# Queries of four token chunks in one layout, loaded in two transfers by heads

## The chip, the cores and the metric

The kernel runs on one core of a Trainium2 chip. The metric is the device time of one execution in microseconds; the time before is the median of 11 runs.

## The reference

A recurrent attention with decay (retention) is followed by a feed-forward layer with a product of two branches, and all of it is computed in float32 by the reference:

```python
for t in range(S):
    state = gamma * state + einsum('bhd,bhe->bhde', k[:, :, t], v[:, :, t])
    y[:, :, t] = scale * einsum('bhd,bhde->bhe', q[:, :, t], state)
x = y.transpose(0, 2, 1, 3).reshape(B * S, H * D)
out = ((x @ w1) * (x @ w2) @ w3) @ w_out
```

There are 4 batches, 8 heads, 768 tokens per batch and a head size of 64, so x is 3072 by 512; w1 and w2 are 512 by 1024, w3 is 1024 by 1024, w_out 1024 by 512. `gamma` is one constant per head.

## The kernel before

The tokens are cut into 24 chunks of 128. Within a chunk the recurrence becomes matmuls: scores (keys against queries, L437), a mask product on DVE (`am`, L442), outputs (values and the running state, L477 to L480), and an update of the state (`kv`, L460 to L469). Heads are taken in four pairs (`NP`), so that two heads of 64 fill the 128 partitions. The decays are put into exponentials: `VS` scales the values as they are cast to float16 into `VP`, `YS` scales the outputs as they are written to `XT` (L485), which is x transposed, ready for the feed-forward matmuls.

The two last weights are multiplied beforehand: `W3O` = w3 @ w_out (`w3_mm_columns`, `w3_mm`), from transposes of w3. Then each block of 256 tokens takes `x @ w1` and `x @ w2` (L508), their product `HT`, and `HT @ W3O` (L534).

The order on every engine is the order in which the program is written; nothing is rearranged later. All loads are issued by SP on one queue, in program order, and most are 512 KB. The order of the loads is: four w3 column blocks and four w_out blocks in turn, four w3 row blocks, then q, k and v of the first pair of chunks (`load_pair(0)`), the four row blocks of w1, q and k of the second pair, a row block of w2, v of the second pair, the rest of w2, and then the chunks from 4 on. `load_pair` puts two neighbouring tokens into one partition, so a contiguous run is 2 x 64 floats, 512 B. With this layout token 2i + t of a pair of chunks lies in partition i; in the first four chunks the order of keys and values within the chunk follows from it (`pair_casts`), and so do the mask `keep2` and the position table `if_i`.

The stretch around the change is written by hand, from L674 to L779. It runs in this order:

- `q_cast(0)` on POOL (L327), then the casts of k (L313) and v (L318), for the first pair, shared by POOL and DVE.
- On PE the rest of `w3_mm` (L293), the query transposes of chunks 0 and 1 (`q_transposes(0)`, L366) with two copies back on DVE (`qT`, L228), the key transposes of chunks 0 and 1 (L421) with copies back into `KP` (L426 and L230, ACT), scores, outputs and state of these chunks.
- On POOL the casts of W1 row blocks 0 and 1 (L687); on ACT the casts of blocks 2 and 3.
- `by_rows` (L724) multiplies the first 256 tokens of `XT` with w1 one row block at a time, first for chunk 0's columns, then for chunk 1's, then for whole blocks. Between blocks 2 and 3 stand the query transposes of chunks 2 and 3 (`q_transposes(1)`), their copies on DVE, and chunk 2's key transposes (`transposes(2)`), the last in the midst of block 3.
- Then scores and outputs of chunks 2 and 3 between the row blocks of w2, the first products `HT`, and a loop over chunks 4 to 23 (`step`), in which a queue of feed-forward units is drawn down by fixed costs.

Tiles are kept in named PSUM banks (`psA0`, `psA1`, `psY`, `psK`, `psT`, three of `psF`), and a new tile under a name waits until the last one is read.

Of the kernel before, what the change touches and what calls it, by code (L numbers as in the profile page):

```python
# [9 lines left out]
FP = mybir.dt.float32  # L10
HP = mybir.dt.float16
AF = mybir.ActivationFunctionType
MULT = mybir.AluOpType.mult
# [5 lines left out]
def kernel(  # L19
# [11 lines left out]
    nc = tc.nc  # L31
    B, H, S, D = q.shape
    C = 128
# [5 lines left out]
    NP = H // 2  # L39
# [21 lines left out]
    def dma_in(dst, src):  # L61
        nc.sync.dma_start(dst, src)  # L62

    chunk_in = {}
    q_in = {}
    pair_in = {}

    def load_pair(m, names="qkv"):

        b, c = divmod(2 * m, NCH)  # L70
        for nm, src in (("q", q), ("k", k), ("v", v)):
            if nm not in names:
                continue
            if nm == "q":
                t = ld.tile([128, 2 * 512], FP, tag="q64", name="q64", bufs=3)
                q_in[m] = t
            else:
                t = new_stage()
                pair_in[nm, m] = t
            dma_in(  # L80
                t[:, :].rearrange("p (h x) -> p h x", x=2 * D),
                src[b, :, c * C : (c + 2) * C, :].rearrange("h (p t) d -> p h (t d)", t=2),
            )

    def load_chunk(n):
        if n >= NSTEP:
            return
        b, c = divmod(n, NCH)
        tiles = []
        if c % 2 == 0:  # L90

            t = ld.tile([128, 2 * 512], FP, tag="q64", name="q64", bufs=3)
            dma_in(
                t[:, :].rearrange("p (h x) -> p h x", x=2 * D),
                q[b, :, c * C : (c + 2) * C, :].rearrange("h (p t) d -> p h (t d)", t=2),
            )
            q_in[n // 2] = t
        for nm, src in (("k", k), ("v", v)):
            t = ld.tile([128, 512], FP, tag=nm + "32", name=nm + "32")
            dma_in(  # L100
                t[:, :].rearrange("p (h d) -> p h d", d=D),
                src[b, :, c * C : (c + 1) * C, :].rearrange("h i d -> i h d"),
            )
            tiles.append(t)
        chunk_in[n] = tiles
# [29 lines left out]
        w3c_st.append(load_w3_columns(i))  # L135
        wo_st.append(load_wo(i))
    w3_st = {f: load_rows(moe_w3, f) for f in range(4, 8)}
    load_pair(0)
    w1_st = [load_rows(moe_w1, d) for d in range(4)]
    load_pair(1, "qk")  # L140
    w2_st = [load_rows(moe_w2, 0)]
    load_pair(1, "v")
    w2_st += [load_rows(moe_w2, d) for d in range(1, 4)]
# [43 lines left out]
    for p in range(NP):  # L187
        nc.scalar.activation(YS[:, p, :], if_f[:, :], AF.Exp, scale=LGP[:, p : p + 1])

    keep2 = const.tile([128, 128], FP, name="keep2")  # L190
    nc.gpsimd.memset(keep2[:, :], 1.0)
    for t in range(2):
        r = slice(t * 64, t * 64 + 64)
        nc.gpsimd.affine_select(
            out=keep2[r, :], in_=keep2[r, :], compare_op=mybir.AluOpType.is_ge, fill=0.0,
            base=-t, pattern=[[1, 2], [2, 64]], channel_multiplier=-2,
        )

    ip2_i = const.tile([128, 2, H], mybir.dt.int32, name="ip2_i")
# [5 lines left out]
    zero(KP[0])  # L205
    zero(KP[1])

    for i in (1, 2):
        nc.gpsimd.memset(VP[i][:, :, :, :].rearrange("p a b c -> p (a b c)").bitcast(FP), 0.0)
    nc.gpsimd.memset(GS[:, :, :], 0.0)  # L210
# [4 lines left out]
    XT = {}  # L215
# [10 lines left out]
    def cast_to(dst, src, on_dve):  # L226
        if on_dve:
            nc.vector.tensor_copy(dst, src)  # L228
        else:
            nc.scalar.copy(dst, src)  # L230
# [11 lines left out]
    def bank(tag, shape, dtype, name):  # L242
        return (ps_t if tag == "psT" else ps_at).tile(shape, dtype, tag=tag, name=name)
# [43 lines left out]
    def w3_mm(f, between=None, at=4):  # L287
        t = w3t.pop(f)
        ps = ps_f.tile([128, DM], FP, tag="psF", name="psW")
        for g in range(8):  # L290
            if g == at and between:
                between()
            nc.tensor.matmul(  # L293
                ps[:, :], lhsT=t[:, g * 128 : (g + 1) * 128], rhs=WO[g // 2][:, g % 2, :],
                start=(g == 0), stop=(g == 7),
            )
        cast_to(W3O[f][:, :], ps[:, :], False)
# [27 lines left out]
    def q_cast(m):  # L325
        q16 = att.tile([128, 1024], HP, tag="q16", name="q16")
        nc.gpsimd.tensor_copy(  # L327
            q16[:, :].rearrange("i (t h d) -> i h t d", t=2, d=D),
            q_in.pop(m)[:, :].rearrange("i (h t d) -> i h t d", t=2, d=D),
        )  # L330
        q16s[m] = q16

    def casts(n):
        if n >= NSTEP:
            return
        k32, v32 = chunk_in.pop(n)
        if n % 2 == 0:
            q_cast(n // 2)
        k16 = att.tile([128, 512], HP, tag="k16", name="k16", bufs=3)
        nc.gpsimd.tensor_copy(k16[:, :], k32[:, :])  # L340
        vp = VP[n % 3]

        for r in range(2):
            nc.gpsimd.tensor_tensor(  # L344
                vp[:, :, r, r * 64 : r * 64 + 64],
                v32[:, :].rearrange("j (p s e) -> j p s e", s=2, e=64)[:, :, r, :],
                VS[:, :].rearrange("j (p s) -> j p s", s=2)[:, :, r].unsqueeze(2).broadcast_to((128, NP, 64)),
                MULT,
            )
        k16s[n] = k16  # L350

    def q_transposes(m, later=False):

        if m >= DT0 // 2:
            return
        q16 = q16s.pop(m)
        if m == 0:
            ps = ps_at.tile([128, NP, 2, 128], HP, tag="psA0", name="psTq")
        elif m == 1:
            ps = ps_at.tile([128, NP, 2, 128], HP, tag="psA1", name="psTq")  # L360
        else:
            ps = ps_f.tile([128, NP, 2, 128], HP, tag="psF", name="psTq")
        for p in range(NP):
            for t in range(2):
                c0 = t * 512 + p * 128
                nc.tensor.transpose(ps[:, p, t, :], q16[:, c0 : c0 + 128], ident16[:, :])  # L366

        def back(c, on_dve=True):
            qT = att.tile([128, NP, 128], HP, tag="qT", name="qT", bufs=4)
            cast_to(  # L370
                qT[:, :, :].rearrange("p a (t i) -> p (a t) i", t=2),
                ps[:, :, :, c * 64 : (c + 1) * 64].rearrange("p a t i -> p (a t) i"), on_dve,
            )
            qTs[2 * m + c] = qT

        if later:
            return back
        back(0)
        back(1)

    def by_dma(n):

# [23 lines left out]
    def transposes(n, tag="psT"):  # L406
        if n >= NSTEP:
            return
        if by_dma(n):
            kT, kp = kTs.pop(n), KP[n % 2]  # L410
            nc.scalar.copy(kp[0:64, :, 0, :], kT[0:64, :, :])  # L411
            nc.scalar.copy(kp[64:128, :, 1, :], kT[64:128, :, :])  # L412
            return
        transposes_front(n, tag)
        transposes_back(n)
# [56 lines left out]
    def outputs(n, tag="psY"):  # L472
        am, vp = ATs.pop(n), VP[n % 3]
        c = n % NCH
        ps = bank(tag, [128, NP, 128], FP, "psY")
        for p in range(NP):
            nc.tensor.matmul(ps[:, p, :], lhsT=vp[:, p, 0, :], rhs=am[:, p, 0, :], start=True, stop=False)  # L477
            nc.tensor.matmul(ps[:, p, :], lhsT=vp[:, p, 1, :], rhs=am[:, p, 1, :], start=False, stop=(c == 0))  # L478
            if c > 0:
                nc.tensor.matmul(ps[:, p, :], lhsT=Tst[0][:, p, :], rhs=queries(n, p), start=False, stop=True)  # L480
        if n % 2 == 0:
            XT[n // 2] = xpool.tile([128, NP, 256], HP, tag="xt", name="xt")

        order = "p a (t i) -> p a t i"
        nc.vector.tensor_tensor(  # L485
            XT[n // 2][:, :, n % 2 * C : (n % 2 + 1) * C].rearrange("p a (i t) -> p a t i", t=2),
            ps[:, :, :].rearrange(order, t=2), YS[:, :, :].rearrange(order, t=2), MULT,
        )


# [138 lines left out]
    def cast_w(W, st, d, on_dve):  # L629
        cast_to(W[d][:, :], st[d][:, :], on_dve)  # L630
# [40 lines left out]
    w3_transpose(5)  # L671
    cast_w3(6, w3_st[6])
    cast_w3(7, w3_st[7])
    q_cast(0)  # L674
    pair_casts(0, False, "k")
    pair_casts(1, False, "k")
    pair_casts(0, False, "v")
# [3 lines left out]
    w3_mm(5, lambda: w3_transpose(7))  # L681
    pair_casts(0, True, "k")
    pair_casts(1, True, "k")
    q_transposes(0)
    pair_casts(0, True, "v")
    for r in (0, 1):
        nc.gpsimd.tensor_copy(W1[r][:, :], w1_st[r][:, :])  # L687
    w3_mm(6, lambda: transposes(0), 3)
    transposes(1, "psK")
    scores(0)  # L690
    cast_w(W1, w1_st, 2, False)

    def chunk1_scores():
        first.append(kv(0, "psT"))
# [2 lines left out]

    first = []
    w3_mm(7, chunk1_scores)
    Tst[0] = first[0]  # L700
    outputs(1, "psT")
    Tst[0] = kv(1, "psK", nc.vector)
    cast_w(W1, w1_st, 3, False)
    q_cast(1)

    ffn = [Ffn(a, b - a) for a, b in zip(bounds, bounds[1:])]
    NT = len(ffn)
# [27 lines left out]
        pair_casts(n, False, "k")  # L735
        pair_casts(n, True, "k", nc.scalar)
    by_rows(W1, ps, 2)
    q_back = q_transposes(1, True)
    q_back(0)
    q_back(1)  # L740
    by_rows(W1, ps, 3, blocks=(0, 3))
    transposes(2)
    by_rows(W1, ps, 3, blocks=(3, 8))
    transposes_front(3, "psK")
    pa = [hold[i // 2][:, i % 2 * 512 : i % 2 * 512 + 512].rearrange("p (a n) -> p a n", a=2) for i in range(4)]
    nc.gpsimd.tensor_copy(W2[0][:, :], w2_st[0][:, :])
# [85 lines left out]
```

## Time and profile before

| | |
|---|---|
| median of 11 runs | 195.01 us (194.67 to 196.93) |
| the profiled execution | 194.85 us |
| its span in the trace | 193.0 us |
| PE busy | 184.1 us (95%) |
| DVE, ACT, POOL busy | 117.4, 99.9, 85.7 us |
| granted TensorE clock | 0.998 |
| moved by DMA | 40.54 MB |

A span runs from the first to the last instruction of the profiled execution, and the 1.85 us that the time is longer lie around it. Lines such as `23.68 1.56 DVE L313 CAST ... x2` give the start and the length in us, the engine, the line of the kernel, the operation, what is written from what, the shape, and how many instructions were merged. A bracket holds the engine's idle time before it and what ended that. A line number can be a helper's (L228 and L230 are DVE's and ACT's copies, L62 issues a load).

### The profile page before, as it was taken

To read this page: it belongs to the slowest core of one execution; us is meant where nothing else is said; L and a number is where in the kernel's file an instruction comes from. 1 tells how busy PE (TensorE), PEld (TensorE's weight loads), DVE (VectorE), ACT (ScalarE), POOL (GpSimd) and SP (SyncE) were. 2 spreads that over 40 slices of the span, in tenths; PEclk is the share of its full clock that TensorE was granted. 3 is DMA by queue.
4 is the path that set the end of the run, shared out by engine and by line. 5 is a ranking of instruction groups with operands and counts; after the bars stand their busy time and mean duration, and the time that the engine had idled before them with its cause. 6 is when DMAs were issued, how large, how long until landed. Compare 5 with 4: busy or idle time off the path is not lost.

```text
span 193.0 us, 4697 instructions
## 1 busy us (share of the span) xinstructions
PE 184.1 (95%) x1777; PEld 139.6 (72%) x1777; DVE 117.4 (61%) x220; ACT 99.9 (52%) x192; POOL 85.7 (44%) x146
## 2 busy tenths in 40 slices
PE   6689999879999999999999999999999999999993
PEld 2335657677797789777877797788777877887752
DVE  3226598599587758656665676565656665753220
ACT  6578565772454464454635463555355545533322
POOL 7600378638872658457153652862426432200000
PEclk9999999999999999999999999999999999999999
DMA  5999999999899999999999999979979931111104
GB/s 194 369 389 395 296 402 323 357 302 201 182 222 221 240 205 239 115 266 219 221 251 251 184 225 218 204 160 267 199 177 209 198 94 21 58 54 54 38 27 156
DMA packets 85031, 40.54 MB, mean 210 GB/s; under 512 B 61329, under 2 KB 80017, under 8 KB 85009
## 3 DMA queue, kind: packets, MB, share of 16 engines
q1 hardware_dynamic: 85008, 40.25, 87.7%
q8 instruction: 14, 0.23, 0.6%
q14 instruction: 9, 0.07, 0.2%
HBM read 29.36 MB, written 6.29 MB: 185 GB/s over the span
## 4 chain that ended last, share of the span: by engine, by line
PE 81%; DMA 10%; POOL 3%; SPq 1%; DVE 1%; issue 1%; ACT 1%; POOLq 0%; DVEq 0%
PE psF L508 39%; PE psO L534 21%; DMA stg<-in_v_dram 5%; DMA stg<-in_moe_w_dram 5%; PE psA L437 5%; PE psY L477 3%; PE psY L478 3%; PE psF L724 2%; PE psY L480 2%; PE psK L460 2%; POOL vp L318 2%; SPq L62 1%; PE psG L508 1%; PE psO L551 1%; PE psG L724 1%
## 5 line engine op out<-in xcount | busy, mean ns | idle before, releaser
L508 PE MATMUL psF<-xt,w 128*128 128x256 f16 (+1 forms) x736 | 85.0, 266 | 0.0
L508 PEld LDWEIGHTS <-w 128*128 128x128 f16 x768 | 68.2, 98 | 7.2
L524 DVE TENSOR_TENSOR ht<-pa,psF 128x256 f16<-128x256 f32 x88 | 36.6, 417 | 22.7 <-PE psF L508 12.8
L518 ACT COPY pa<-psF 128x256 f32<-128x256 f32 x84 | 31.3, 373 | 33.7 <-PE psF L508 33.3
L442 DVE TENSOR_TENSOR am<-psA,keep 128x512 f16<-128x512 f32 x48 | 31.0, 685 | 20.9 <-PE psA L437 20.8
L534 PE MATMUL psO<-w3o,ht 128*128 128x512 f16 x184 | 43.3, 379 | 0.0
L469 POOL TENSOR_TENSOR t<-s,GS 128x512 f16<-128x512 f32 x15 | 19.3, 1283 | 33.2 <-DVE s L468 33.1
L539 ACT ACTIVATE osb<-psO 128x512 f32<-128x512 f32 x23 | 13.8, 599 | 35.6 <-PE psO L534 35.6
L534 PEld LDWEIGHTS <-ht 128*128 128x128 f16 x184 | 17.9, 98 | 16.9 <-DVE ht L773 0.2
L344 POOL TENSOR_TENSOR vp<-v,VS 128x256 f16<-128x256 f32 x40 | 23.8, 614 | 8.6 <-DMA v<-in_v_dram 5.0
L327 POOL CAST q<-q 128x1024 f16<-128x1024 f32 x12 | 12.7, 1056 | 28.6 <-DMA q<-in_q_dram 28.6
L485 DVE TENSOR_TENSOR xt<-psY,YS 128x512 f16<-128x512 f32 x24 | 17.8, 742 | 4.0 <-PE psY L480 3.6
L477 PE MATMUL psY<-am,vp 128*128 128x128 f16 x96 | 16.8, 219 | 0.6 <-ACT kp L230 0.4
L478 PE MATMUL psY<-am,vp 128*128 128x128 f16 x96 | 16.7, 219 | 0.6 <-DVE vp L318 0.6
L437 PEld LDWEIGHTS <-kp 128*128 128x128 f16 x192 | 12.5, 98 | 4.9 <-DVE kp L228 0.4
L340 POOL CAST k<-k 128x512 f16<-128x512 f32 x20 | 12.2, 611 | 5.9 <-DMA v<-in_v_dram 2.2
L468 DVE TENSOR_TENSOR s<-psK,t 128x512 f32<-128x512 f32 x16 | 11.0, 689 | 3.0 <-PE psK L460 2.7
L251 DVE COPY w3t<-psW 128x1024 f16<-128x1024 f16 x8 | 5.5, 690 | 10.6 <-PE psW L259 8.2
L411 ACT COPY kp<-kT 64x512 f16<-64x512 f16 x17 | 10.5, 620 | 1.9 <-DMA kT<-k 1.5
L437 PE MATMUL psA<-qTd,kp 128*128 128x128 f16 x144 | 11.1, 219 | 0.0
L480 PE MATMUL psY<-qTd,t 128*128 128x128 f16 x60 | 10.8, 219 | 0.0
L412 ACT COPY kp<-kT 64x512 f16<-64x512 f16 x17 | 10.5, 617 | 0.4
(82 smaller groups left out, 190.2 us busy)
## 6 DMA issues: line engine op xcount, KB each, us to landing
stg<-in_moe_w_dram SPq DMA_DIRECT2D x16, 512.0 KB, 7.8
q<-in_q_dram SPq DMA_DIRECT2D x12, 512.0 KB, 5.7
out_dram<-osb SPq DMA_DIRECT2D x23, 256.0 KB, 3.9
k<-in_k_dram SPq DMA_DIRECT2D x20, 256.0 KB, 5.2
v<-in_v_dram SPq DMA_DIRECT2D x20, 256.0 KB, 5.5
stg<-in_moe_w_out_dram SPq DMA_DIRECT2D x4, 512.0 KB, 7.8
stg<-in_k_dram SPq DMA_DIRECT2D x2, 512.0 KB, 10.7
stg<-in_v_dram SPq DMA_DIRECT2D x2, 512.0 KB, 8.2
```

Of the source, the lines that this page charges most:

```text
L344: nc.gpsimd.tensor_tensor(vp[:, :, r, r * 64 : r * 64 + 64], v32[:, :].rearrange("j (p s e) -> j p s e", s=2, e=64)[:, :, r, :], VS[:, :]. ...
L437: nc.tensor.matmul(ps[:, i, r, :], lhsT=kp[:, p, r, :], rhs=queries(n, p), start=True, stop=True)
L442: nc.vector.tensor_tensor(am[:, half * 2 : half * 2 + 2, :, :].rearrange("j p s i -> j (p s) i"), ps[:, :, :, :].rearrange("j p s i -> j ( ...
L469: eng.tensor_tensor(t16[:, :, :], s32[:, :, :], GS[:, :, :], MULT)
L477: nc.tensor.matmul(ps[:, p, :], lhsT=vp[:, p, 0, :], rhs=am[:, p, 0, :], start=True, stop=False)
L478: nc.tensor.matmul(ps[:, p, :], lhsT=vp[:, p, 1, :], rhs=am[:, p, 1, :], start=False, stop=(c == 0))
L480: nc.tensor.matmul(ps[:, p, :], lhsT=Tst[0][:, p, :], rhs=queries(n, p), start=False, stop=True)
L485: nc.vector.tensor_tensor(XT[n // 2][:, :, n % 2 * C : (n % 2 + 1) * C].rearrange("p a (i t) -> p a t i", t=2), ps[:, :, :].rearrange(orde ...
L508: nc.tensor.matmul(ps[:, i * w : (i + 1) * w], lhsT=W[d][:, (f + i) * 128 : (f + i + 1) * 128], rhs=XT[self.tok0 // TB][:, d, c0 : c0 + w] ...
L518: nc.scalar.copy(self.pa[f][:, :], ps[:, :])
L524: nc.vector.tensor_tensor(self.HT[:, f : f + TB // self.width, :].rearrange("p f n -> p (f n)"), self.pa.pop(f)[:, :], ps[:, :], MULT,)
L534: nc.tensor.matmul(psO[:, :], lhsT=self.HT[:, f, tb * 128 : (tb + 1) * 128], rhs=W3O[f][:, :], start=(f == 0), stop=(f == 7),)
```

## The change

The queries of chunks 0 to 3 (512 tokens) are loaded by two transfers, `load_q4(0)` for heads 0 to 3 and `load_q4(1)` for heads 4 to 7, four neighbouring tokens in a partition, so a contiguous run is 1 KB. Both stand ahead of the first k; the second pair's q load goes. The first half is cast on POOL, the second on ACT (`q4_cast`). Eight PE transposes for each half (`q4_transposes`) stand where `q_transposes(0)` stood, with a copy back for each chunk and half: six on DVE, and on ACT those of chunks 2 and 3 for the second half. Query columns within a chunk now come in another order, so the mask `keep2` and the decay table take it (`YS4`, made by two POOL copies), and `outputs` writes `XT` with a stride of 4 instead of 2. `q_transposes(1)` and `q_cast(1)` go; `transposes(2)` now stands ahead of the whole of W1 row block 3; the cast of W1 row block 2 stands behind `w3_mm(7)`; chunk 0's key transposes use bank `psA0`.

```diff
--- before.py
+++ after.py
@@ -82,6 +82,15 @@
                 src[b, :, c * C : (c + 2) * C, :].rearrange("h (p t) d -> p h (t d)", t=2),
             )
 
+    def load_q4(half):
+
+        t = ld.tile([128, 2 * 512], FP, tag="q64", name="q256", bufs=3)
+        dma_in(
+            t[:, :].rearrange("p (h x) -> p h x", x=4 * D),
+            q[0, half * 4 : half * 4 + 4, 0 : 4 * C, :].rearrange("h (p t) d -> p h (t d)", t=4),
+        )
+        q_in["half", half] = t
+
     def load_chunk(n):
         if n >= NSTEP:
             return
@@ -135,9 +144,11 @@
         w3c_st.append(load_w3_columns(i))
         wo_st.append(load_wo(i))
     w3_st = {f: load_rows(moe_w3, f) for f in range(4, 8)}
-    load_pair(0)
+    load_q4(0)
+    load_q4(1)
+    load_pair(0, "kv")
     w1_st = [load_rows(moe_w1, d) for d in range(4)]
-    load_pair(1, "qk")
+    load_pair(1, "k")
     w2_st = [load_rows(moe_w2, 0)]
     load_pair(1, "v")
     w2_st += [load_rows(moe_w2, d) for d in range(1, 4)]
@@ -187,13 +198,14 @@
     for p in range(NP):
         nc.scalar.activation(YS[:, p, :], if_f[:, :], AF.Exp, scale=LGP[:, p : p + 1])
 
+
     keep2 = const.tile([128, 128], FP, name="keep2")
     nc.gpsimd.memset(keep2[:, :], 1.0)
     for t in range(2):
         r = slice(t * 64, t * 64 + 64)
         nc.gpsimd.affine_select(
             out=keep2[r, :], in_=keep2[r, :], compare_op=mybir.AluOpType.is_ge, fill=0.0,
-            base=-t, pattern=[[1, 2], [2, 64]], channel_multiplier=-2,
+            base=-t, pattern=[[1, 4], [4, 32]], channel_multiplier=-2,
         )
 
     ip2_i = const.tile([128, 2, H], mybir.dt.int32, name="ip2_i")
@@ -205,6 +217,12 @@
     zero(KP[0])
     zero(KP[1])
 
+    YS4 = const.tile([128, NP, 128], FP, name="YS4")
+    for r in range(2):
+        nc.gpsimd.tensor_copy(
+            YS4[:, :, r * 64 : r * 64 + 64].rearrange("p a (l i) -> p a l i", l=2),
+            YS[:, :, :].rearrange("p a (l i h) -> p a l i h", l=2, h=2)[:, :, :, :, r],
+        )
     for i in (1, 2):
         nc.gpsimd.memset(VP[i][:, :, :, :].rearrange("p a b c -> p (a b c)").bitcast(FP), 0.0)
     nc.gpsimd.memset(GS[:, :, :], 0.0)
@@ -330,6 +348,33 @@
         )
         q16s[m] = q16
 
+    def q4_cast(half, on_act):
+        q16 = att.tile([128, 1024], HP, tag="q16", name="q16")
+        (nc.scalar.copy if on_act else nc.gpsimd.tensor_copy)(
+            q16[:, :].rearrange("i (t h d) -> i h t d", t=4, d=D),
+            q_in.pop(("half", half))[:, :].rearrange("i (h t d) -> i h t d", t=4, d=D),
+        )
+        q16s["half", half] = q16
+
+    def q4_transposes(half, tag):
+
+        q16 = q16s.pop(("half", half))
+        ps = bank(tag, [128, 2, 4, 128], HP, "psTq")
+        for p in range(2):
+            for t in range(4):
+                c0 = t * 256 + p * 128
+                nc.tensor.transpose(ps[:, p, t, :], q16[:, c0 : c0 + 128], ident16[:, :])
+
+        def back(n, on_dve=True):
+            if n not in qTs:
+                qTs[n] = att.tile([128, NP, 128], HP, tag="qT", name="qT", bufs=4)
+            cast_to(
+                qTs[n][:, half * 2 : half * 2 + 2, :].rearrange("p a (t i) -> p (a t) i", t=4),
+                ps[:, :, :, n * 32 : n * 32 + 32].rearrange("p a t i -> p (a t) i"), on_dve,
+            )
+
+        return back
+
     def casts(n):
         if n >= NSTEP:
             return
@@ -349,34 +394,24 @@
             )
         k16s[n] = k16
 
-    def q_transposes(m, later=False):
+    def q_transposes(m):
 
         if m >= DT0 // 2:
             return
         q16 = q16s.pop(m)
-        if m == 0:
-            ps = ps_at.tile([128, NP, 2, 128], HP, tag="psA0", name="psTq")
-        elif m == 1:
-            ps = ps_at.tile([128, NP, 2, 128], HP, tag="psA1", name="psTq")
-        else:
-            ps = ps_f.tile([128, NP, 2, 128], HP, tag="psF", name="psTq")
+        ps = ps_f.tile([128, NP, 2, 128], HP, tag="psF", name="psTq")
         for p in range(NP):
             for t in range(2):
                 c0 = t * 512 + p * 128
                 nc.tensor.transpose(ps[:, p, t, :], q16[:, c0 : c0 + 128], ident16[:, :])
 
-        def back(c, on_dve=True):
+        for c in range(2):
             qT = att.tile([128, NP, 128], HP, tag="qT", name="qT", bufs=4)
-            cast_to(
+            nc.vector.tensor_copy(
                 qT[:, :, :].rearrange("p a (t i) -> p (a t) i", t=2),
-                ps[:, :, :, c * 64 : (c + 1) * 64].rearrange("p a t i -> p (a t) i"), on_dve,
+                ps[:, :, :, c * 64 : (c + 1) * 64].rearrange("p a t i -> p (a t) i"),
             )
             qTs[2 * m + c] = qT
-
-        if later:
-            return back
-        back(0)
-        back(1)
 
     def by_dma(n):
 
@@ -481,10 +516,10 @@
         if n % 2 == 0:
             XT[n // 2] = xpool.tile([128, NP, 256], HP, tag="xt", name="xt")
 
-        order = "p a (t i) -> p a t i"
+        order, t, ys = "p a (t i) -> p a t i", (4 if n < 4 else 2), (YS4 if n < 4 else YS)
         nc.vector.tensor_tensor(
-            XT[n // 2][:, :, n % 2 * C : (n % 2 + 1) * C].rearrange("p a (i t) -> p a t i", t=2),
-            ps[:, :, :].rearrange(order, t=2), YS[:, :, :].rearrange(order, t=2), MULT,
+            XT[n // 2][:, :, n % 2 * C : (n % 2 + 1) * C].rearrange("p a (i t) -> p a t i", t=t),
+            ps[:, :, :].rearrange(order, t=t), ys[:, :, :].rearrange(order, t=t), MULT,
         )
 
 
@@ -671,7 +706,8 @@
     w3_transpose(5)
     cast_w3(6, w3_st[6])
     cast_w3(7, w3_st[7])
-    q_cast(0)
+    q4_cast(0, False)
+    q4_cast(1, True)
     pair_casts(0, False, "k")
     pair_casts(1, False, "k")
     pair_casts(0, False, "v")
@@ -681,14 +717,20 @@
     w3_mm(5, lambda: w3_transpose(7))
     pair_casts(0, True, "k")
     pair_casts(1, True, "k")
-    q_transposes(0)
+    back = [q4_transposes(0, "psA1"), q4_transposes(1, "psY")]
+    back[0](0)
+    back[1](0)
+    for n in range(1, 4):
+        back[0](n)
+    back[1](1)
     pair_casts(0, True, "v")
     for r in (0, 1):
         nc.gpsimd.tensor_copy(W1[r][:, :], w1_st[r][:, :])
-    w3_mm(6, lambda: transposes(0), 3)
+    w3_mm(6, lambda: transposes(0, "psA0"), 3)
     transposes(1, "psK")
+    for n in range(2, 4):
+        back[1](n, False)
     scores(0)
-    cast_w(W1, w1_st, 2, False)
 
     def chunk1_scores():
         first.append(kv(0, "psT"))
@@ -697,11 +739,11 @@
 
     first = []
     w3_mm(7, chunk1_scores)
+    cast_w(W1, w1_st, 2, False)
     Tst[0] = first[0]
     outputs(1, "psT")
     Tst[0] = kv(1, "psK", nc.vector)
     cast_w(W1, w1_st, 3, False)
-    q_cast(1)
 
     ffn = [Ffn(a, b - a) for a, b in zip(bounds, bounds[1:])]
     NT = len(ffn)
@@ -735,12 +777,8 @@
         pair_casts(n, False, "k")
         pair_casts(n, True, "k", nc.scalar)
     by_rows(W1, ps, 2)
-    q_back = q_transposes(1, True)
-    q_back(0)
-    q_back(1)
-    by_rows(W1, ps, 3, blocks=(0, 3))
     transposes(2)
-    by_rows(W1, ps, 3, blocks=(3, 8))
+    by_rows(W1, ps, 3)
     transposes_front(3, "psK")
     pa = [hold[i // 2][:, i % 2 * 512 : i % 2 * 512 + 512].rearrange("p (a n) -> p a n", a=2) for i in range(4)]
     nc.gpsimd.tensor_copy(W2[0][:, :], w2_st[0][:, :])
```

## The prediction

> **What bounds the kernel now.** I read the busy table and the 40 slices first. PE is busy for 184.1 of 193.0 us at full granted clock, and its gaps lie in the first quarter. A table of busy time by stretch shows where: after the load-bound start, the last real gaps are between 30 and 41 us.
>
> ```profile
> 30.00:35.00 5.00, 4.91 (x61) 3.93 (x58) 3.24 (x6) 2.71 (x4) 3.57 (x5) 1.00 1.15 316
> 35.00:40.00 5.00, 3.40 (x36) 2.58 (x36) 3.88 (x8) 4.29 (x8) 4.13 (x7) 1.00 1.06 375
> 45.00:50.00 5.00, 5.00 (x47) 3.14 (x45) 3.86 (x7) 1.34 (x3) 3.80 (x5) 1.00 1.01 230
> ```
>
> The columns after the length are PE, PEld, DVE, ACT, POOL, clock, DMA share and GB/s. From 41 us on PE is full: the work between `scores(3)` (40.59) and the first output matmul (46.59) adds up to about 6.0 us, with no hole. So the end moves by what the point near 41 us moves by, and by nothing else. The chain of waits shows what leads to that point:
>
> ```profile
> 16.19 9.75 DMA stg<-in_v_dram
> 26.11 1.15 POOL vp L318 x2
> ...
> 30.26 1.05 POOL w L687
> 31.36 0.51 PE psF L724 x6
> ...
> 35.44 0.38 PE psT L421 x4
> ```
>
> So v of chunks 0 and 1 lands (26.1), W1 row block 0 is cast, the row-block matmuls of L724 start, and chunk 2's key transposes (L421, called T(2) below) come at 35.44. For the price of a landing I take ACT's timeline, where a cast follows a wait for its DMA:
>
> ```profile
> 9.30 1.05 ACT L230 CAST wo<-stg 128x1024 f16<-128x1024 f32 x1 [0.25 <-DMA stg<-in_moe_w_out_dram]
> 10.79 1.05 ACT L230 CAST w3h<-stg 128x1024 f16<-128x1024 f32 x1 [0.44 <-DMA stg<-in_moe_w_dram]
> 12.08 1.05 ACT L230 CAST wo<-stg 128x1024 f16<-128x1024 f32 x1 [0.24 <-DMA stg<-in_moe_w_out_dram]
> 17.49 1.05 ACT L230 CAST w3h<-stg 128x1024 f16<-128x1024 f32 x1 [0.23 <-DMA stg<-in_moe_w_dram]
> 34.68 1.26 ACT L313 CAST k<-stg 64x512 f16<-64x512 f32 x2 [2.27 <-DMA stg<-in_k_dram]
> 35.92 0.58 ACT L426 COPY kp<-psT 64x512 f16<-64x512 f16 x1
> ```
>
> All these loads are 512 KB. A block with 4 KB runs (wo, rows of w3) lands 1.28 us after the one before it (10.79 to 12.08), a w3 column block with 1 KB runs 1.49 us (9.30 to 10.79). For 512 B runs I use POOL and DVE:
>
> ```profile
> 21.93 1.04 POOL L327 CAST q<-q 128x1024 f16<-128x1024 f32 x1 [13.40 <-DMA q<-in_q_dram]
> 23.61 1.36 POOL L313 CAST k<-stg 64x512 f16<-64x512 f32 x2 [0.64 <-DMA stg<-in_k_dram]
> 32.96 1.06 POOL L327 CAST q<-q 128x1024 f16<-128x1024 f32 x1 [0.68 <-DMA q<-in_q_dram]
> 23.68 1.56 DVE L313 CAST k<-stg 64x512 f16<-64x512 f32 x2
> 25.17 0.73 DVE L228 COPY qT<-psTq 128x512 f16<-128x512 f16 x2
> 26.04 1.17 DVE L318 TENSOR_TENSOR vp<-stg,VS 64x256 f16<-64x256 f32 x2
> 30.24 1.59 DVE L485 TENSOR_TENSOR xt<-psY,YS 128x512 f16<-128x512 f32 x2
> ```
>
> k follows q by 1.68 (23.61 - 21.93), and by 1.72 in the second pair (34.68 - 32.96). The last w3 row is put at 17.49 + 2 x 1.28 = 20.05, so q itself took 1.88. From 23.68 to 33.1 DVE has only 0.14 us idle: it is the pacer of that stretch, and k of the first pair starts it.
>
> **Part 1, the loads.** Ahead of k stood one q with 512 B runs; now two halves with 1 KB runs stand there. Nearest row: the w3 column block, 1.49. First half 20.05 + 1.49 = 21.54 (was 21.93), second 23.03. k of chunks 0 and 1, its v and all W1 rows land later by 2 x 1.49 - 1.88 = 1.10: k at 24.71, v at 27.2. The old second q (1.88) then goes, so k of chunks 2 and 3 and what follows land earlier by 0.78: 33.9 instead of 34.68. Bounds for one half: 1.28 (the 4 KB row; shift 0.68) and 1.88 (the 512 B row; shift 1.88). I take 1.49, since run length is the same.
>
> The Trainium skill, in "DMA: Bandwidth & Descriptors", section "Specifications", gives 512 B as the smallest transfer for line rate, which speaks against a gain from longer runs. The rows here differ, 1.49 against 1.68 to 1.88. By the page the first shift would be one whole old load, 1.88, and the total some 0.8 us more than mine.
>
> **Part 2, DVE.** The k casts move from 23.68 to 24.78 and end at 26.27. Then six copies of 128x256 stand where two of 128x512 stood. The forms view has 415 ns for 512 elements, and 690 ns for the 1024 of w3t; so 275 ns per 512, and 0.28 us for one of 256. The old pair took 0.73, so the second began 0.315 after the first, an overlap of 0.10; a small copy then spaces 0.18, and six take 1.18. Bounds: 1.1, and 2.0 if each is spaced like a 512 one. I take 1.18, the line through two rows of the same kind of copy. vp starts at 27.45 (v is there at 27.2) instead of 26.04: the shift is 1.10 + 0.45 - 0.14 of old idle = 1.41. The two mask products, the state product, the next two mask products and the two xt products keep their order behind it, so xt of chunk 1 ends at 31.83 + 1.41 = 33.24. xt with stride 4 in its output and the reordered mask have the old sizes; xt costs 742 against 685 for the dense mask product, so a further 0.06 each is the bound, nothing the choice, and below nothing is excluded as the elements are no fewer.
>
> **Part 3, PE and the row blocks.** The second pass of L724 started at 31.88, just after xt's end at 31.83. From there 2.22 us of row blocks ran to 34.10. Then came the eight query transposes (0.45), three matmuls of W1 row block 3 (0.33), and a 0.57 us rest of waiting for chunk 2's keys until 35.44. All three no longer stand ahead of T(2): 1.35 us off. New T(2): 34.10 + 1.41 = 35.51, against 35.44. The keys are cast by 33.9 + 0.7 = 34.6, so they no longer decide. W1 blocks 0 and 1 on POOL: v at 27.2, six vp 4.15, casts end 32.4 and 33.4; block 1 is needed at about 33.75. This cover is 0.35 us; if it goes, the row blocks wait for POOL by as much. W1 block 3's other matmuls now follow T(2) entirely; PE reaches `scores(2)` at 37.0 as before (37.01, waiting for kp).
>
> **Part 4, the wait for kp.** ACT copied kp at 35.92, when both T(2) (done 35.82) and its own k casts (done 35.94) let it. Now the k casts are over by 35.3 and T(2) ends 35.89: kp at 36.0, +0.1. DVE then runs kp, pa, mask product, two vp and mask product back to back to 40.2, which gated outputs of chunk 2. None of them changes.
>
> **Part 5, at nothing.** ACT's cast of the second half waits for 23.03 and ends near 24.1. Behind it are the W3O casts of blocks 4 and 5 (21.65 and 23.82 before, now about 24.1 and 24.7); the bank of the first is wanted by `w3_mm(7)`, which began at 26.78, later still now. PE's second eight transposes (0.45) wait until about 24.15 against 24.07; PE then has idle time before chunk 0's keys at 25.6. ACT's two copies for chunks 2 and 3 (373 ns for 128x256) come behind kp of chunk 1, near 29 to 29.7, and the bank psY is wanted near 30.2. Cover 0.5 us. The two YS4 copies on POOL, at most 0.61 each by the vp row, lie in its 13.4 us of idleness. W1 block 2's cast behind W3O of block 7 ends near 33, and is needed near 34.6. On SP the later loads keep their order and only come sooner; SP waits for no new buffer, since the first q tile is cast before 22.7.
>
> **Sum.** Loads +1.10, copies +0.45, old idle -0.14, removed ahead of T(2) -1.35: +0.06, through ACT about +0.1. The profiled execution took 194.85 with a span of 193.0; I expect a span of 193.1 and 194.95, on the median of 195.01 that is 195.1.
>
> **Rivals.** (a) Faster: the halves land at the 4 KB price. Then T(2) comes 0.42 earlier, and with cheaper copies, or a smaller lag of v, toward the floor set by the keys at 34.6: at most -0.7, so 194.3 to 194.7. For it: the source of each head is one contiguous 128 KB stretch. Against: the only 1 KB row says 1.49, and POOL's W1 casts would bind after 0.35. (b) Slower: each 256-element copy on DVE is spaced like a 512 one, 0.315: +0.82, 195.9. It decides from about 0.26 us each. For it: runs are only 32 elements. Against: 1024 elements cost just 1.66 times 512. (c) Slower: 1 KB runs of q gain nothing over 512 B: shift 1.88, +0.85, 195.9. Against it are the w3 rows. (d) The move saves nothing because loads bound it anyway is my forecast itself: one transfer late at the head eats what is taken from the middle.
>
> **Numbers.** Forecast, within 0.3% (0.58 us, about what a measurement of this kernel can tell from no change): 0.45. (a) beyond -0.58: 0.18; (b) 0.2; (c) 0.17, so slower 0.37. The range takes (a) to -0.7 and (b) or (c) with a part of the other, to +1.2: 194.3 to 196.2.
>
> **What would show it.** Right: k's first POOL cast near 24.7 and vp on DVE near 27.5; six qT copies of about 0.28; the second pass of L724's successor near 33.3; T(2) near 35.5 with no wait for keys; PE without holes from 41. (a) shows T(2) before 35, (b) qT copies over 0.35, (c) k at 25.4 or later. Wrong altogether: holes in PE after 46 us, or outputs of chunk 0 waiting for ACT's copies out of psY.

## The result, and the profile after: slower by 1.7 us

The changed kernel took 196.73 us (median of 12 runs, 196.19 to 197.71), the kernel before 195.05 in the runs beside it: a ratio of 1.0077 with an interval of 1.0059 to 1.0095. The forecast of 195.1 is missed, and the range of 194.3 to 196.2 does not hold the median. The profiled execution took 196.22 us with a span of 194.4, so its span is 1.4 longer than that of before.

The table of busy time by stretch, in the columns named in the prediction:

```profile
30.00:35.00 5.00, 3.81 (x52) 2.97 (x50) 4.98 (x7) 3.24 (x6) 4.07 (x7) 1.00 1.13 332
35.00:40.00 5.00, 4.68 (x51) 3.89 (x47) 3.06 (x6) 3.58 (x8) 4.04 (x6) 1.00 1.05 376
40.00:45.00 5.00, 4.54 (x59) 4.13 (x60) 4.94 (x9) 3.19 (x5) 0.19 (x1) 1.00 1.02 214
45.00:50.00 5.00, 4.63 (x50) 3.35 (x48) 4.97 (x7) 1.21 (x4) 4.14 (x5) 1.00 1.09 241
```

The stretch from 40 to 45 us before the change, which the prediction doesn't show:

```profile
40.00:45.00 5.00, 4.81 (x65) 4.47 (x63) 4.97 (x8) 3.10 (x5) 2.09 (x3) 1.00 1.09 242
```

PE has lost 1.1 us between 30 and 35 (3.81 against 4.91), and 0.27 and 0.37 in the two stretches after 40. It also lost 1.22 between 25 and 30 (3.62 against 4.84) and has 1.28 more between 35 and 40, where work that came late is done. DVE is full from 30 to 35 and from 40 to 50. The chain of waits names it as well:

```profile
12.93 12.45 DMA stg<-in_k_dram
25.85 0.72 DVE k L331
26.57 0.63 DVE qT L246 x4
...
41.66 0.47 DVE xt L520
...
44.70 1.84 DVE vp L336 x2
46.54 0.14 issue
46.68 0.22 PE psY L513
```

Before, the chain ran from the landing of v through POOL and PE. Now it runs from the landing of k through DVE, and DVE's work from 38 to 46.5 us stands on it too. Between 32.46 and 38.25 the chain goes over the landing of a weight block instead, which ends just as DVE is done with its copy of kp (37.80 + 0.43). So the pair of xt products at 32.00 isn't on the chain; who waits for that pair is read from PE's timeline below. The timelines of POOL and ACT, with the loads:

```profile
16.79 1.05 ACT L248 CAST w3h<-stg 128x1024 f16<-128x1024 f32 x1 [0.23 <-DMA stg<-in_moe_w_dram]
20.89 1.04 POOL L353 CAST q<-q 128x1024 f16<-128x1024 f32 x1 [11.68 <-DMA q<-in_q_dram]
22.33 1.05 ACT L353 CAST q<-q 128x1024 f16<-128x1024 f32 x1 [1.95 <-DMA q<-in_q_dram]
25.43 1.62 POOL L331 CAST k<-stg 64x512 f16<-64x512 f32 x2 [3.51 <-DMA stg<-in_k_dram]
```

The first line is a w3 row, cast as soon as it lands; in the profile of before it stood at 17.49, so all loads run 0.70 us earlier in this execution. The halves are there at 20.89 and 22.33, and k only 3.1 us after the second. DVE's timeline:

```profile
25.40 1.17 DVE L331 CAST k<-stg 64x512 f16<-64x512 f32 x2 [2.45 <-DMA stg<-in_k_dram]
26.50 1.26 DVE L246 COPY qT<-psTq 128x256 f16<-128x256 f16 x6
27.79 1.18 DVE L336 TENSOR_TENSOR vp<-stg,VS 64x256 f16<-64x256 f32 x2
32.00 2.46 DVE L520 TENSOR_TENSOR xt<-psY,YS 128x512 f16<-128x512 f32 x2
...
37.80 0.43 DVE L246 COPY kp<-psT 64x512 f16<-64x512 f16 x1 [1.87 <-ACT kp L461]
39.57 0.76 DVE L336 TENSOR_TENSOR vp<-stg,VS 64x256 f16<-64x256 f32 x2
41.65 1.31 DVE L520 TENSOR_TENSOR xt<-psY,YS 128x512 f16<-128x512 f32 x1
```

Two of these lines as they were before the change:

```profile
38.31 1.17 DVE L318 TENSOR_TENSOR vp<-stg,VS 64x256 f16<-64x256 f32 x2
40.79 0.75 DVE L485 TENSOR_TENSOR xt<-psY,YS 128x512 f16<-128x512 f32 x1
```

The pair of xt products takes 2.46 us instead of 1.59, and one alone 1.31 instead of 0.75. On PE's timeline that is what the second pass of the row blocks waits for:

```profile
34.51 0.49 PE L766 MATMUL psF<-xt,w 128*128 128x128 f16 x6 [0.55 <-DVE xt L520]
36.70 0.39 PE L456 MATMUL psT<-ident,k 128*128 128x128 f16 x4
...
46.68 0.22 PE L513 MATMUL psY<-am,vp 128*128 128x128 f16 x1 [0.37 <-DVE vp L336]
47.96 2.32 PE L569 MATMUL psO<-w3o,ht 128*128 128x512 f16 x10
```

The second pass and the first output matmul before the change:

```profile
31.88 0.49 PE L724 MATMUL psF<-xt,w 128*128 128x128 f16 x6
46.59 3.62 PE L534 MATMUL psO<-w3o,ht 128*128 128x512 f16 x16
```

The second pass begins 2.63 us later than before, T(2) 1.26 later, and the first output matmul 1.37 later. The last is the whole growth of the span.

### The profile page after: what moved, and what is told of

It is laid out like the page before. It is cut to its first block, busy times and chain, and to the rows that moved or that the text cites. A ratio compares the mean times of both kernels' runs of the same rounds, so it can differ in the third digit from the quotient of the medians.

```text
span 194.4 us, 4700 instructions
## 1 busy us (share of the span) xinstructions
PE 184.0 (95%) x1777; PEld 139.9 (72%) x1777; DVE 118.7 (61%) x222; ACT 100.8 (52%) x195; POOL 85.2 (44%) x147
## 4 chain that ended last, share of the span: by engine, by line
PE 75%; DMA 14%; DVE 6%; SPq 2%; issue 1%; ACT 0%
PE psF L543 39%; PE psO L569 20%; DMA stg<-in_k_dram 6%; PE psA L472 5%; DMA stg<-in_moe_w_out_dram 4%; DMA stg<-in_moe_w_dram 3%; PE psY L513 3%; PE psY L512 2%; PE psY L515 2%; DVE am L477 2%; PE psK L495 2%; DVE vp L336 2%; SPq L62 2%; PE psO L586 1%; DVE stg L246 1%
## 5 line engine op out<-in xcount | busy, mean ns | idle before, releaser
L559 DVE TENSOR_TENSOR ht<-pa,psF 128x256 f16<-128x256 f32 x88 | 36.6, 417 | 22.0 <-PE psF L543 12.0
L520 DVE TENSOR_TENSOR xt<-psY,YS 128x512 f16<-128x512 f32 x24 | 19.9, 839 | 3.9 <-PE psY L515 3.6
L345 POOL CAST q<-q 128x1024 f16<-128x1024 f32 x10 | 10.6, 1056 | 12.9 <-DMA q<-in_q_dram 12.9
```

What stands on the lines that cost most here:

```text
L520: nc.vector.tensor_tensor(XT[n // 2][:, :, n % 2 * C : (n % 2 + 1) * C].rearrange("p a (i t) -> p a t i", t=t), ps[:, :, :].rearrange(orde ...
L559: nc.vector.tensor_tensor(self.HT[:, f : f + TB // self.width, :].rearrange("p f n -> p (f n)"), self.pa.pop(f)[:, :], ps[:, :], MULT,)
```

## The experiments

My theory after the result: the larger part is the write of xt, whose stride of 4 float16 elements costs more than its stride of 2 did; the smaller is k, which lands later than priced. The rival: xt is slow for another reason (its four-dimensional form, the strided read of the decays, a neighbour on the memory), or doesn't matter, and the loads make all of the loss. All ratios are against the kernel before, run beside each on the same chip.

**Stride 4 alone in the kernel before.** `t = (4 if n < 4 else 2)` in the three views of the xt product, nothing else; the rows of the first 512 tokens then come out in another order than the reference's.

> The kernel before, with only the write of xt for chunks 0 to 3 changed to a stride of 4 (same number of elements; the rows of the first 512 tokens come out in another order than the reference's). Theory A: xt takes 1.3 us instead of 0.74; the pair's end and the second pass of the row blocks move by about +0.9, chunk 2's key transposes only by about +0.3, since they waited 0.57 us for keys there; time +0.3 to +0.8 us, 195.3 to 195.9. Rival B: xt's price is hidden, within 0.2 us of the kernel before.

197.17 us, ratio 1.0093 (1.0060 to 1.0127): this single view costs about as much as the whole change. Its runs spread widely (195.79 to 198.14); the fastest is 1.06 us above the fastest of the kernel before beside it (194.73). DVE's timeline shows the same pair as in the changed kernel:

```profile
32.09 2.45 DVE L485 TENSOR_TENSOR xt<-psY,YS 128x512 f16<-128x512 f32 x2
```

It is also more than I expected. The xt products of chunks 2 and 3 (1.32 and 1.30 us) begin at 42.91 and 50.24, and from 40 to 50 us DVE is as full in this kernel as after the change (4.94 of 5.00 us in both halves), so chunk 2's at least is paid as well. In this execution all loads came some 1.5 us later, so only places relative to ACT's cast of the w3 row can be compared: T(2) is 0.65 and the first output matmul 1.18 later. The xt pair itself begins 0.38 later by this measure, so not all of the 0.65 is the stride's; the 0.53 between T(2) and the output matmul is about what chunk 2's xt grew by.

**The forms by themselves.** The kernel before, with extra DVE and ACT operations at its end, each three times over; its total time says nothing.

```python
nc.vector.tensor_tensor(m16[:, :, :], mp[:, :, :], YS[:, :, :], MULT)      # L813
# L814 to L817: the same written with stride 2, 4, 8, 16
nc.vector.tensor_tensor(v(m16, T, 4), v(mp, T, 4), v(YS, T, 4), MULT)      # L818: dense, same form
nc.vector.tensor_tensor(v(m32, O, 4), v(mp, T, 4), v(YS, T, 4), MULT)      # L820: float32, stride 4
# L821: dense write, PSUM read with stride 32; L824: ACT, float16, stride 4
```

`v(x, O, t)` is the view with a stride of t elements in memory, `v(x, T, t)` the view with the same dimensions that goes through memory in order.

> The kernel before, and behind its end extra products on DVE on idle tiles, three times each, 128x512 of float32 from PSUM by float32 from SBUF: float16 written with strides 1, 2, 4, 8, 16; float16 written dense in the four-dimensional order of stride 4; float32 written with strides 2 and 4; float16 written dense with PSUM read at a stride of 32. Two ACT copies with strided writes. The total time says nothing. Theory A: 0.69, 0.74, 1.25 or more for stride 4, and as much or more for 8 and 16; if the order of the dimensions and not the stride is the cause, the dense four-dimensional form takes 1.25 too. Float32 at stride 2 has the same 8 bytes between elements as float16 at stride 4: 1.25 if bytes decide, 0.74 if elements decide.

The groups of instructions, kept apart by form (busy, mean ns of one, idle before):

```profile
L813 DVE TENSOR_TENSOR m<-mps,YS 128x512 f16<-128x512 f32 x3 | 2.1, 691 | 3.8 <-ACT m L824 3.8
L814 DVE TENSOR_TENSOR m<-mps,YS 128x512 f16<-128x512 f32 x3 | 2.2, 732 | 0.1
L815 DVE TENSOR_TENSOR m<-mps,YS 128x512 f16<-128x512 f32 x3 | 3.9, 1296 | 0.1
L816 DVE TENSOR_TENSOR m<-mps,YS 128x512 f16<-128x512 f32 x3 | 7.3, 2427 | 0.1
...
L818 DVE TENSOR_TENSOR m<-mps,YS 128x512 f16<-128x512 f32 x3 | 2.1, 692 | 0.1
...
L821 DVE TENSOR_TENSOR m<-mps,YS 128x512 f16<-128x512 f32 x3 | 2.0, 672 | 0.0
```

A float16 write costs 691 ns dense, 732 at stride 2, 1296 at stride 4, 2427 at stride 8 (2293 at 16). The form with the same dimensions and a dense write has 692, so it is the step in memory and not the shape. These operations stand behind the kernel's end, and stride 4 costs there what it costs in the kernel (1.31), so no neighbour is needed for it either. A read of PSUM with stride 32 costs no more than a dense one (672). So the stride can be moved from the write to the read.

**The changed kernel with a dense write in token order.** The three views of the xt product are turned round (`cols` is the same part of `XT` as before), and the two POOL copies lay the decay table in token order:

```diff
+        if n < 4:
+            nc.vector.tensor_tensor(
+                cols.rearrange("p a (i t) -> p a i t", t=4),
+                ps[:, :, :].rearrange("p a (t i) -> p a i t", t=4),
+                YS4[:, :, :].rearrange("p a (i t) -> p a i t", t=4), MULT,
+            )
+            return
...
```

> The changed kernel, with xt of chunks 0 to 3 written dense in token order: the product reads PSUM at a stride of 32 elements (the form that took 0.67 us by itself), the decay table is laid in token order, and nothing else changes, the output stores included. Theory A (the write's stride is most of what the forecast missed): xt pair 1.35 instead of 2.46 us, the second pass of the row blocks 1.1 earlier, PE without the holes for xt of chunks 2 and 3 either; time down by 1.2 to 1.5 us, 195.2 to 195.5, which is what the forecast had but for the later landing of the first k. Rival B (the later landing of k is most of it): down by under 0.5 us.

195.55 us, ratio 1.0016 (0.9995 to 1.0037). DVE's and PE's timelines:

```profile
32.02 1.44 DVE L521 TENSOR_TENSOR xt<-psY,YS 128x512 f16<-128x512 f32 x2
```

```profile
35.70 0.39 PE L455 MATMUL psT<-ident,k 128*128 128x128 f16 x4
```

xt begins at 32.0 as in the changed kernel and takes 1.44 instead of 2.46; T(2) comes at 35.70 instead of 36.70. With this one edit 1.2 us of the loss are gone by the ratios (1.0077 to 1.0016), and all the rest of the change is still in it. That settles the larger part.

**The same, without token order.** Here xt of chunks 0 to 3 was written dense in the order in which PSUM has it, and the output rows were put right by four stores of 32 rows each for the first 512 tokens.

> The changed kernel, with x of chunks 0 to 3 written in the order in which it comes out of PSUM (no stride in the write), and the four output stores that hold these tokens put each row in its place (four stores of 32 rows instead of one). Theory A, the stride of 4 in xt's write is what was missed: the two xt of chunks 0 and 1 take 0.7 us each instead of 1.3, the second pass of the row blocks moves from 34.5 to about 33.4, chunk 2's key transposes from 36.7 to about 35.6, and the time falls by 0.9 to 1.2 us, to 195.5 to 195.8. Rival B, the later landing of the first k is what was missed and xt has slack: the time falls by under 0.3 us.

199.02 us, ratio 1.0183 (1.0151 to 1.0215). The xt pair fell to 1.44 us here too, and T(2) came at 35.86 instead of 36.70, but the stores cost more than that brought. SP's timeline and POOL's:

```profile
51.39 5.74 SPq L580 DMA_DIRECT2D out_dram<-osb  x8
```

```profile
64.50 1.04 POOL L345 CAST q<-q 128x1024 f16<-128x1024 f32 x1 [4.63 <-DMA q<-in_q_dram]
```

Eight stores hold SP's queue for 5.74 us, where the two whole ones of the changed kernel took 1.76, and the loads of later chunks stand behind them. POOL waits 4.63 us for a q; in the changed kernel it waits 2.88 for the same one, which is cast 1.18 earlier. From 75 to 85 us PE is busy for 7.98 of 10 us, where it was full. Neither expectation saw it; of xt's price the total of this run says nothing.

**The load order alone.** The kernel before, with the second pair's q (512 B runs) loaded ahead of the first k.

```diff
-    load_pair(0)
+    load_pair(0, "q")
+    load_pair(1, "q")
+    load_pair(0, "kv")
...
-    load_pair(1, "qk")
+    load_pair(1, "k")
```

> The kernel before, with only the load of the second pair's q moved ahead of the first k (512 B runs, all else as it was). By the forecast's method: the first k and v land 1.88 us later, DVE's chain moves by 1.74, the second pass of the row blocks to 33.6, and with the query transposes and three matmuls of row block 3 still ahead chunk 2's key transposes go from 35.44 to 36.6: +1.2 us, 196.2. If k lands later still than by one load (the instruction transfer near 22 us falls into it, as in the changed kernel), +1.5 to +2. Theory A alone says nothing against either; if the loads are hidden anyway, within 0.3 us of the kernel before.

196.41 us, ratio 1.0065 (1.0039 to 1.0091), +1.3 where my steps say +1.2. POOL's timeline:

```profile
26.10 1.61 POOL L315 CAST k<-stg 64x512 f16<-64x512 f32 x2 [3.36 <-DMA stg<-in_k_dram]
```

The way from loads to DVE to T(2) is confirmed: T(2) stands at 36.77 and 36.6 was expected. But against the cast of the w3 row k is 2.71 later where one q load (1.88) stands in front of it, so here too some 0.8 more than priced. Loads that ran 0.22 earlier in this execution and a pair of k casts of 1.17 instead of 1.56 us gave most of that back, so the close agreement in the total is in part luck.

**k ahead of the queries.** The kernel with the dense write, k loaded before the two halves, casts and transposes put in that order, both halves cast on POOL and W1 row block 0 on ACT.

> x5_dense_write, with k of the first pair loaded ahead of the two q halves, its casts and its transposes ahead of q's on POOL, DVE and PE, both halves cast by POOL, and the cast of W1 row block 0 on ACT. If the first k's landing is what is left (theory B for the rest), vp on DVE starts when v lands, 0.5 us sooner than with q first, and chunk 2's key transposes near 35.0: 194.4 to 195.0, a little faster than before. If the loads are not what is left: as x5_dense_write, within 0.2 us.

195.68 us, ratio 1.0031 (1.0015 to 1.0047): nothing gained. DVE has k at 23.16, then waits 1.86 us for the second half's transposes, and vp starts where it did without the edit:

```profile
27.79 1.24 DVE L336 TENSOR_TENSOR vp<-stg,VS 64x256 f16<-64x256 f32 x2
```

In the order of DVE's program the copies of both halves stand ahead of vp, so the last of these loads decides, whichever it is.

**The kernel before with dense writes.** All xt written dense, read from PSUM with stride 64.

> The kernel before, with xt of all chunks written dense (PSUM read at a stride of 64, table in token order): 0.67 instead of 0.74 us each. The pair of chunks 0 and 1 ends 0.14 earlier, but chunk 2's keys are waited for there, and PE is full later: within 0.2 us of the kernel before. It is the fair partner of x5_dense_write and x6_k_first: if it is faster by more, their gain over the kernel before is partly the write's.

194.94 us, ratio 0.9983 (0.9965 to 1.0001): within 0.2 us. Stride 2 had cost 0.04 us per product in the forms above, which the total doesn't show.

**The same, with T(2) moved ahead.** The old loads, but the second pair's k before its q; T(2) ahead of row block 3 and of the second query transposes; DVE's copy of the second product ahead of the query copies.

> A version meant to beat both: x7_before_dense (the old loads, two tokens per partition), with k of the second pair loaded ahead of its q, chunk 2's key transposes ahead of W1 row block 3 and of the second query transposes, and DVE's copy of the second product ahead of the query copies. If what made chunk 2 late before was its k landing behind q (the 0.57 us wait at 35.44 and the transposes ahead of it), chunk 2's key transposes go to about 34.1, the first mask product of chunk 2 from 37.6 to about 37.0, and the time falls by 0.4 to 0.6 us against x7_before_dense: 194.3 to 194.6. If something else holds that stretch (v landing at 37.8, or DVE's own sum), within 0.2 us of x7_before_dense.

194.93 us, ratio 0.9988 (0.9971 to 1.0005): no gain that can be told. The profile is of an execution of 196.18 us in which all loads ran 1.0 later than in the profile of before, so it isn't typical; PE's timeline shows where the wait went in it:

```profile
36.80 0.62 PE L370 MATMUL psTq<-ident,q 128*128 128x128 f16 x8 [0.97 <-POOL q L331]
```

Now the query transposes wait, because q is the load that lands last. No version here clearly beats the kernel before.

## Why the prediction was wrong, step by step

**The step that failed** is in part 2: "a further 0.06 each is the bound, nothing the choice". The term of xt was taken as nothing for the two products on the way to T(2). It measured 0.87 for the pair (2.46 against 1.59) and 0.56 for a single one, and with a dense write in its place most of the loss is gone. The bound was a line through two rows, dense and stride 2, and nothing in the trace showed a stride of 4. It was no bound: from stride 1 to 2 a product grows by 41 ns, from 2 to 4 by 564, from 4 to 8 by 1131. I should have kept the upper end open, as "costs as stride does", twice 742; two products on the path then give 195.1 + 2 x 0.74 = 196.6 for that end.

The sum against the profile, from before to after: DVE's k casts start 1.72 later (forecast 1.10), vp 1.75 later (1.41), xt begins 1.76 later (1.41) and ends 2.63 later (1.41), T(2) comes 1.26 later (0.07). The miss of 1.19 at T(2) is 0.87 of xt and 0.35 of the way up to it, less 0.03 of the row blocks.

**Loads.** The halves were priced right: from the w3 cast at 16.79 and two rows of 1.28, they took 1.54 and 1.44 against 1.49. So rival (c), longer runs gain nothing, falls, though the sign that the prediction gave for it, k at 25.4 or later, did show, with another cause. With it falls what was worked out from the Trainium skill's page "DMA: Bandwidth & Descriptors", section "Specifications": the rows of 1 KB runs are shorter than those of 512 B, and the measurement decides.

What was missed is k. Against the w3 cast its cast on POOL is 2.52 later and not 1.10; the sum above shows 1.72 because all loads ran 0.70 earlier. Of the spacing behind the first q (before) and the second half (after), k had 1.68 and v 2.50 in the one, k 3.07 and v about 1.9 in the other. In the one-microsecond windows of DMA the two traces have one transfer of 20 KB on the instruction queue, before at 22 to 23 us and after at 21 to 22. That it delayed v before and k after, and k is what starts DVE, fits both, but it is argued. Its share of 7.5% of 16 engines in that microsecond is an estimated 1.2 us of one engine. Two more observations speak for it. With k loaded ahead of the queries the transfer stands at 22 to 23 us, and there the second half of q is cast 2.64 us after the first, where the changed kernel had 1.44:

```profile
22.85 1.03 POOL L353 CAST q<-q 128x1024 f16<-128x1024 f32 x1 [0.31 <-DMA q<-in_q_dram]
25.49 1.04 POOL L353 CAST q<-q 128x1024 f16<-128x1024 f32 x1 [1.60 <-DMA q<-in_q_dram]
```

And in the three profiles of the changed order (the changed kernel, the dense write, the four stores) DVE starts on k at 25.40, 25.43 and 25.59, though the w3 cast stood at 16.79, 17.31 and 17.12: k's landing doesn't just follow the loads ahead of it. Against the transfer as the cause stand the two profiles whose loads ran latest (stride 4 alone, and T(2) moved ahead): the transfer is there at 22 to 23 and 21 to 22, and q, k and v still follow one another by 1.84, 1.66 and 1.82. So the cause of k's delay stays open, and no run here took this transfer away. A part was given back: DVE's pair of k casts took 1.17 and not 1.56.

**Copies.** Six took 1.26 against 1.18. Rival (b), 0.315 each, falls.

**The 1.35 us taken from ahead of T(2)** came as forecast: 2.19 us from the second pass to T(2) against 2.22, with no wait for the keys. The saving is real and was eaten by what came before it.

**After T(2)** part 4 said of DVE's work that "none of them changes". From T(2) to the first output matmul it was 11.26 us against 11.15, but only since two changes met: the vp pair took 0.76 instead of 1.17, and xt of chunk 2 took 1.31 instead of 0.75. With DVE full, that is where PE's wait of 0.37 us at 46.68 comes from, of the kind that the prediction named as "wrong altogether". So the end did not move only by what the point near 41 us moved by: T(2) is 1.26 later, the first output matmul 1.37. The kernel with the dense write has no such hole (PE 5.00 of 5.00 us from 45 to 50).

**What is left without xt** is +0.3 us by the ratio of the dense version, with an interval of -0.1 to +0.7, where the rest of my sum said +0.1. Against its fair partner, the kernel before with dense writes, it is 0.6 (195.55 against 194.94, run beside each other). In its profile T(2) is 0.26 later than before and the first output matmul 0.61 (47.20); between the two PE waits 0.75 us for POOL's vp at 39.47, where it had waited 0.38 for a copy on ACT. So by all its other terms the change was about what rival (d) says, or a little worse: one transfer late at the head eats what is taken from the middle.

## What to carry to other kernels

A token layout in the load comes back as a stride somewhere: put it on the PSUM read, and keep float16 writes dense or at stride 2. A new form of a known instruction has no price until it is measured, and two rows of smaller strides are no bound for the next. Where an engine needs a group of loads before it can go on, only the last to land counts; reordering within the group brought nothing here, and neither did the one reordering tried behind it.

## What the runs showed of the hardware

The cost of a strided write on DVE (128x512, from float32, written as float16: 691, 732, 1296, 2427 and 2293 ns at strides 1, 2, 4, 8, 16) goes by type too: in float32 it was 681 ns at stride 2 and 1058 at stride 4. ACT's cast to float16 at stride 4 took 1292 ns against 587 dense in the kernel.

The Trainium skill, in "Advanced Engine Details and Errata", section "Memory Cachelines", asks for at least two hits on a 16-byte line to absorb its latency, and says that the tolerated stride goes by type. The float32 rows agree (8 bytes apart 681, 16 bytes apart 1058); the float16 rows do not, for at stride 4 two elements still share such a line and the write took 1296; the measurement decides.

Reads differ: PSUM with stride 32 costs no more than in order (672 ns), while the float32 table in SBUF read with the same stride made it 1018.
